# Softmax steps, kept V blocks and w1 row products between two passes over the KV cache

## The chip, the cores and the metric

One core of one Trainium2 chip runs the whole program in one launch. The metric is the device time of that execution in microseconds (us). Five engines have their own instruction streams: PE (matmul; its weight loads are shown as PEld), DVE, ACT, POOL, and SP, which here does nothing but issue loads from DRAM. Stores are issued by POOL.

## The reference

Two attention blocks and two dense blocks alternate on one token, and then the gradients of all of it are taken. The parameters of the two attention blocks are the same arrays, and so are those of the dense blocks:

```python
def _A_ref(x, k_cache, v_cache, wq, wo):          # Hq=32 heads, 4 KV heads, 65536 positions, Dh=128
    q = (x @ wq) ...                               # x: [1, 1, 1024]
    scores = einsum("bhqd,bhkd->bhqk", q, k) * (Dh ** -0.5)
    o = einsum("bhqk,bhkd->bhqd", softmax(scores), v)
    return o.reshape(...) @ wo
def _B_ref(x, w1, b1, w2, b2):                     # 1024 -> 3584 -> 1024
    return relu(x @ w1 + b1) ** 2 @ w2 + b2
...
x = x + _A_ref(_layernorm(x), ...); x = x + _B_ref(_layernorm(x), ...)
x = x + _A_ref(_layernorm(x), ...); x = x + _B_ref(_layernorm(x), ...)
_out, _vjp = jax.vjp(_f, A_x, A_k_cache, A_v_cache, A_wq, A_wo, B_w1, B_b1, B_w2, B_b2)
return (_out, *_vjp(grad_out))
```

All arrays are bf16. K and V are 67 MB each, and the gradients of K and V are as large. The output is right when the values agree; nothing about order is asked for.

## The kernel before

**Four passes over K and V.** The caches do not fit on the chip, so K and V are read once in each of four passes: pass 1 is the attention of the first block, pass 2 that of the second block (`attn_fwd`, with `p` = 0 and 1), pass 3 the backward attention of the second block (`attn_bwd3`, `p` = 2), and pass 4 (`attn_bwd4`, `p` = 3) the backward attention of the first block together with the stores of dK and dV. Between passes lie dense stretches, in which a chain of small steps (output product `wo`, layer norm, `w1`, and so on) must be done before the next pass can use its result.

**The arena.** One SBUF tile of 20 slots of 1 MB holds everything that is loaded. Eight of them (`plane`) come to hold the softmax weights E of two layers and four groups; the other twelve take blocks of K and V, `wo`, `wq`, `w1` and `w2`. `Slot` hands out a free slot when the program is built, `take_pair` a pair for a load of 2 MB. SP issues the loads in the order of the program, and each waits until the last reader of its slot is done; the load behind it in SP's queue waits too.

**Items.** A pass runs over 256 items: 8 chunks of 128 positions each, 256 KB of K and of V. A block (`hb`) is 4 items, 1 MB. `pipeline` walks over the steps and at each step does the stages that are due, each with its lag: in pass 2 K is transposed at lag 0 (`kT`), scores at lag 2 (`kS`), and V is used at lag 36 (`v8`). A unit is 16 items. After the scores of a unit come its softmax steps, made by `stats`, each put some steps later by `after(n, fn)`: `lows` (row minimum, DVE), `turn` (transpose, PE), `low` (DVE), `spread` (PE), `exps` (DVE and ACT), and four times `exp2` (two heads of exponentials each, ACT). `unit_end` folds the unit into the running sum, `group_sum` and `group_out` make the output of the last unit of a group. In pass 3 V is transposed at lag 0 (`vT`), multiplied by dO at lag 2 (`vS`), and K is used at lag 13 (`k8`).

**Kept blocks.** At the end of a pass the first blocks that the next pass needs stay in their slots (`KV["keep"]`, 7 blocks of V from pass 2 to pass 3, 28 items). Four of the seven are blocks that pass 2 has done before its last three: `early_turn` transposes them in place right after `v8` has read them (L1129 to L1134; 16 items), with the copies out of PSUM by ACT and DVE in turn, so that `vT` of pass 3 has nothing to do for them (`is_turned`).

**Between passes 2 and 3.** `g_wo` multiplies by `wo` (L519), `ln_fwd` normalises (L222 to L246), with transposes of `w1` chunk 0 put between its steps by `turn_between`. Then `w1` is worked through in seven chunks of 512 columns (`ch_load`, 1 MB each, 1 KB rows), five of which are loaded ahead. One round of the loop for chunk s is: `ch_fwd(s)`, 32 matmuls and two DVE steps that give `dhb`; `ch_bwd(s-1)`, 20 matmuls; `ch_spread(s)`, 4 matmuls and an ACT copy that spread `dhb` over the partitions; `ch_turn(s+1)`, four times 5 transposes with a copy each (three on ACT, one on DVE; 8 transposes for the last chunk); `ch_dots(s)`, three row products on DVE (L1730); `ch_free(s)` and the next load into that slot. After the rounds come `ln_bwd`, the product with `wo` rows, and pass 3.

The order of instructions on PE, DVE and ACT is the order in the program inside `tc.manual_schedule`.

Of the kernel before, what the change touches and what calls it, by code (L numbers as in the profile page):

```python
# [16 lines left out]
P = 128  # L17
# [3 lines left out]
def kernel(  # L21
# [94 lines left out]
    nc.vector.memset(onesd_f[:], 1.0 / D)  # L116
# [105 lines left out]
    def ln_fwd(x, name, between=lambda n: None, eps=eps_t):  # L222
        s = tmp.tile([P, 1], F32, name="ln_s")
        nc.vector.reduce_sum(out=s[:], in_=x[:], axis=AX.X)
        between(0)
        mean = bcast_sum(s[:], 1, mean=True)
        between(1)
        xc = tmp.tile([P, DC], F32, name="ln_xc")
        negmean = tmp.tile([P, 1], F32, name="ln_negmean")
# [6 lines left out]
        var = bcast_sum(ss[:], 1, mean=True)  # L236
        between(2)
        rstd = vec.tile([P, 1], F32, name=name + "_rstd")
        nc.scalar.activation(out=rstd[:], in_=var[:], func=ACTF.Sqrt, bias=eps[:], scale=1.0)
        nc.vector.reciprocal(out=rstd[:], in_=rstd[:])  # L240
        n = vec.tile([P, DC], F32, name=name + "_n")
        nc.vector.tensor_scalar(out=n[:], in0=xc[:], scalar1=rstd[:, 0:1], scalar2=None, op0=ALU.mult)
        nb = vec.tile([P, DC], BF, name=name + "_nb")
        nc.vector.tensor_copy(out=nb[:], in_=n[:])
        between(3)
        return n, nb, rstd  # L246

    def ln_bwd(dn, n, rstd, between=lambda: None):
# [3 lines left out]
        nc.vector.tensor_tensor(out=pr[:], in0=dn, in1=n[:], op=ALU.mult)  # L252
        nc.vector.reduce_sum(out=st[:, 1:2], in_=pr[:], axis=AX.X)
# [3 lines left out]
        nc.vector.tensor_scalar(out=negm[:], in0=tot[:], scalar1=-1.0, scalar2=None, op0=ALU.mult)  # L257
# [651 lines left out]
    def gsl(g):  # L909
        return slice(g * R, (g + 1) * R)  # L910
# [89 lines left out]
    def attn_fwd(p, L, on_group, bg, end=()):  # L1000
# [56 lines left out]
        def stats(g, su, S, pm):  # L1057
# [52 lines left out]
            for n, fn in ((1, lows), (3, turn), (4, low), (6, spread), (7, exps), (7, exp2(0)), (8, exp2(2)), (9, exp2(4)), (10, exp2(6))):  # L1110
                after(n, fn)

        def v8(g, c8):
# [4 lines left out]
            if c8 % SU == SU // 2 and su != first_su[g]:  # L1118
                t = tmp.tile([P, R], F32, name="o_t")
                nc.vector.tensor_tensor(out=t[:], in0=state[("o", g)][:], in1=state[("al", g, su)][:], op=ALU.mult)  # L1120
                state[("ot", g)] = t
# [7 lines left out]
            if p == 1 and ("v", g, c8 // J) in early_turn:  # L1129
                pt = ps_tr()  # L1130
                for i in range(8):
                    nc.tensor.transpose(pt[:, i, :], vb8[:, i, :], ident_b[:, :])
                evac(vb8[:, :, :], pt[:, :, :], kind="kt" if c8 // 8 % 2 else "kta")
                KV["next"].add(("v", g, c8))  # L1134
# [3 lines left out]
        def unit_end(g, su, ps_o):  # L1138
            on = spool.tile([P, R], F32, name="oacc", tag="oacc", bufs=3)
            rs = state.pop(("rs", g, su))  # L1140
            if su == first_su[g]:
                nc.vector.tensor_copy(out=on[:], in_=ps_o[:, 0, :])
                z2 = rs
            else:
                al = state.pop(("al", g, su))
                nc.vector.tensor_tensor(out=on[:], in0=ps_o[:, 0, :], in1=state.pop(("ot", g))[:], op=ALU.add)
# [4 lines left out]
            state[("o", g)] = on  # L1151
            state[("z", g)] = z2
            if su == last_su[g]:
                after(2, lambda: group_sum(g, z2))
                after(3, lambda: group_out(g, su, on))

        def group_sum(g, z2):
            state["pz"] = bcast_sum(z2[:], R)

        def group_out(g, su, on):  # L1160
            nc.vector.reciprocal(out=L["rZ"][:, gsl(g)], in_=state["pz"][:])
            nc.vector.tensor_tensor(out=L["oT"][:, gsl(g)], in0=on[:], in1=L["rZ"][:, gsl(g)], op=ALU.mult)
            nc.vector.tensor_copy(out=L["oTb"][:, gsl(g)], in_=L["oT"][:, gsl(g)])
# [7 lines left out]
        early_turn = set(k for k in TOUCH[p][:-3] if k in KV["keep"])  # L1171
# [586 lines left out]
    ahead = 0  # L1758
    while ahead < 5 and FREE:
        ch_load(ahead)  # L1760
        ahead += 1
    with tc.manual_schedule(engines=ORDERED):
        run(g_wo(L3, x3, lastg[1], ps_mv, PRE["wo3"]))

        def turn_between(n):
            for s, j, dve in {0: [(0, 0, 0)], 1: [], 2: [(0, 1, 1)], 3: [(0, 2, 0), (0, 3, 1), (1, 0, 0)]}[n]:
                ch_turn(s, [j], {j: dve})
        L4["n"], L4["nb"], L4["rstd"] = ln_fwd(x3, "L4", turn_between, eps4)
        ps_dn = ps_bg([P, DC, 64])
        for s in range(NCH):  # L1770
# [3 lines left out]
            if s < NCH - 1:  # L1774
                ch_spread(s)
                ch_turn(s + 1, [0, 1, 2] if s else [1, 2])
                ch_dots(s)
                ch_turn(s + 1, [3])
            ch_free(s)
            if ahead < NCH:  # L1780
                ch_load(ahead)
                ahead += 1
# [173 lines left out]
```

## Time and profile before

| what | us |
|---|---|
| three timed executions | 1941.15, 1941.16, 1943.75 (median 1941.16) |
| the profiled execution, first to last instruction (span) | 1938.1 |
| busy in it: PE / DVE / ACT / POOL | 1585.2 / 1170.3 / 1044.9 / 142.2 |
| moved by the DMA engines | 787.63 MB, 406 GB/s over the span |

The profiled execution has no other time of its own than its span; the 3 us to the median of the timed runs lie before its first and after its last instruction. In the views, a row of the timeline gives the start in us from the span's start, how long it took, engine, line, operation, what it writes and reads, and in brackets the idle time of the engine before it and what ended that. A row of the windows gives for a stretch its length, the busy time of each engine with the number of instructions, the granted clock of PE, the busy share of the 16 DMA engines (1 and a little over is full) and GB/s. The dense stretch between passes 1 and 2 lies near 345 to 410 us, that between passes 2 and 3 near 740 to 786 us, that between passes 3 and 4 near 1120 to 1220 us.

### The profile page before, as it was taken

Reading aid. Unit: us, or ns where it says so; the run is one execution under the profiler, and the core shown is the slowest. Engines: PE = TensorE matmul, PEld = TensorE weight load, DVE = VectorE, ACT = ScalarE, POOL = GpSimd, SP = SyncE. Lnnn points to the kernel's source line nnn. Section 1 sums busy time; section 2 is a strip of 40 time slices with the busy share of each in tenths; the row PEclk is TensorE's granted clock in tenths of the full one; section 3 lists DMA queues with packets and bytes.
Section 4 is the critical chain, followed back from the end, with each engine's and each line's share of the span. In section 5 each row is a group of like instructions: output and inputs, shape, how many; then the busy total and the mean of one; then the engine's idle time right before and its main releaser. Section 6 shows DMA issues by size and latency. Waiting matters only on the chain. (4 is left out here: it accounts for less than half of the span.)

```text
span 1938.1 us, 66986 instructions
## 1 busy us (share of the span) xinstructions
PE 1585.2 (82%) x30199; PEld 1301.4 (67%) x30199; DVE 1170.3 (60%) x2453; ACT 1044.9 (54%) x1617; POOL 142.2 (7%) x321
## 2 busy tenths in 40 slices
PE   6878778688777888977787898889997987697987
PEld 6878777678777877877776886555554654454554
DVE  5655555255555554545454567777775886685876
ACT  3444334245433545445363455766875885575775
POOL 0000000000000000000000001121111211121211
PEclk9999899689999999998899999898997998797998
DMA  9999999999999998999999988999999999899998
GB/s 393 427 425 425 429 427 415 391 407 423 427 425 429 428 422 309 377 425 429 426 424 421 408 314 308 425 424 389 425 424 413 419 424 424 345 419 397 424 422 352
DMA packets 107149, 787.63 MB, mean 406 GB/s; under 512 B 9440, under 2 KB 16622, under 8 KB 42222
## 3 DMA queue, kind: packets, MB, share of 16 engines
q1 hardware_dynamic: 82782, 617.65, 77.2%
q0 software_dynamic: 24080, 165.70, 20.5%
q8 instruction: 236, 3.87, 0.7%
q14 instruction: 51, 0.42, 0.1%
HBM read 617.62 MB, written 165.69 MB: 404 GB/s over the span
## 5 line engine op out<-in xcount | busy, mean ns | idle before, releaser
L164 DVE COPY kt<-ps_tr 128x1024 bf16<-128x1024 bf16 x724 | 496.3, 688 | 429.0 <-PE ps_tr L1024 244.0
L161 ACT CAST arena<-ps_gg 128x1024 bf16<-128x1024 f32 x457 | 444.4, 1011 | 185.0 <-PE ps_gg L1426 137.9
L1024 PE MATMUL ps_tr<-ident_b,arena 128*128 128x128 bf16 x3840 | 308.2, 225 | 36.9 <-DMA arena<-in_A_k_cache_dram 27.5
L161 ACT COPY kt<-ps_tr 128x1024 bf16<-128x1024 bf16 x164 | 171.0, 1046 | 186.1 <-PE ps_tr L1216 103.3
L164 DVE CAST arena<-ps_gg 128x1024 bf16<-128x1024 f32 (+2 forms) x186 | 222.2, 1195 | 77.1 <-PE ps_gg L1426 34.5
L1024 PEld LDWEIGHTS <-arena 128*128 128x128 bf16 x3840 | 232.9, 101 | 44.7 <-DMA arena<-in_A_k_cache_dram 30.3
L1126 PE MATMUL ps_acc<-arena 128*128 128x64 bf16 (+4 forms) x4096 | 205.6, 196 | 60.2 <-DMA arena<-in_A_v_cache_dram 45.1
L1426 PE MATMUL ps_gg<-GG,xt 64*128 64x512 bf16 x1024 | 210.6, 409 | 43.3 <-DVE arena L164 28.3
L1345 PE MATMUL ps_tr<-ident_b,arena 128*128 128x128 bf16 x1824 | 177.4, 232 | 33.7 <-DMA arena<-in_A_v_cache_dram 30.7
L1126 PEld LDWEIGHTS <-arena 128*128 128x128 bf16 x4096 | 159.9, 100 | 66.1 <-DMA arena<-in_A_v_cache_dram 48.7
L1042 PE MATMUL ps_sc<-L_qpad,kt 128*128 128x64 bf16 (+7 forms) x3584 | 183.0, 194 | 16.3 <-issue 8.3
L1107 ACT ACTIVATE arena<-S_sb,L_negm 128x128 bf16<-128x128 f32 x256 | 165.5, 1002 | 55.7 <-DVE L_negm L1092 42.2
L1216 PE MATMUL ps_tr<-ident_b,arena 128*128 128x128 bf16 x1920 | 154.3, 226 | 44.3 <-DMA arena<-in_A_v_cache_dram 43.5
L1345 PEld LDWEIGHTS <-arena 128*128 128x128 bf16 x1824 | 116.8, 103 | 90.7 <-issue 55.2
L1042 PEld LDWEIGHTS <-kt 128*128 128x128 bf16 x3584 | 152.6, 100 | 20.2 <-issue 8.8
L1216 PEld LDWEIGHTS <-arena 128*128 128x128 bf16 x1920 | 117.1, 101 | 48.8 <-DMA arena<-in_A_v_cache_dram 46.1
L1457 PEld LDWEIGHTS <-arena 128*128 128x128 bf16 x2048 | 92.2, 101 | 57.8 <-issue 39.9
L1107 ACT ACTIVATION_READ_ACCUMULATOR arena<-S_sb,L_negm 128x1 f32 x256 | 127.9, 500 | 0.0
L1426 PEld LDWEIGHTS <-xt 64*128 64x128 bf16 x1024 | 64.5, 94 | 90.1 <-issue 52.3
L587 ACT ACTIVATE mv_t<-mv_t 128x1024 bf16<-128x1024 bf16 x96 | 102.1, 1065 | 35.8 <-DVE mv_t L598 35.8
L1382 PE MATMUL ps_sc<-DOB,kt 128*128 128x64 bf16 (+3 forms) x1824 | 112.3, 197 | 0.1
L1270 PE MATMUL ps_acc<-dsT,arena 128*128 128x64 bf16 (+7 forms) x2048 | 103.1, 194 | 11.3 <-DMA arena<-in_A_k_cache_dram 7.8
(317 smaller groups left out, 2154.0 us busy)
## 6 DMA issues: line engine op xcount, KB each, us to landing
arena<-in_A_k_cache_dram SPq DMA_DIRECT2D x82, 2048.0 KB, 21.7
arena<-in_A_v_cache_dram SPq DMA_DIRECT2D x79, 2048.0 KB, 21.7
out_dram<-arena POOLq DMA_DIRECT2D x149, 1024.0 KB, 16.2
arena<-in_A_v_cache_dram SPq DMA_DIRECT2D x84, 1024.0 KB, 14.2
arena<-in_A_k_cache_dram SPq DMA_DIRECT2D x84, 1024.0 KB, 14.6
arena<-in_A_wo_dram SPq DMA_DIRECT2D x22, 1024.0 KB, 19.6
arena<-in_B_w_dram SPq DMA_DIRECT2D x21, 1024.0 KB, 9.2
arena<-in_A_wq_dram SPq DMA_DIRECT2D x18, 1024.0 KB, 18.0
```

Source lines behind the costliest of these rows:

```text
L161: nc.scalar.copy(out=out, in_=in_)
L164: nc.vector.tensor_copy(out=out, in_=in_)
L587: nc.scalar.activation(out=t[:, :], in_=t[:, :], func=ACTF.Copy, accum_out=y[:, kc:kc + 1])
L1024: nc.tensor.transpose(pt[:, i, :], kb8[:, i, :], ident_b[:, :])
L1042: nc.tensor.matmul(state["ps_s"][:, s:s + w, :].rearrange("p a b -> p (a b)"), lhsT=kt[:, i, :], rhs=L["qpad"][:, g, 0:w, :].rearrange("p ...
L1107: nc.scalar.activation(out=E(p, g, c0, SU)[:, :, h], in_=S[:, h, :], func=ACTF.Exp, bias=L["negm"][:, g, su, h:h + 1], scale=SCALE, accum_ ...
L1126: nc.tensor.matmul(ps_o[:, 0:w, :], lhsT=vb8[:, i, :], rhs=E(p, g, c, w), start=(c % SU == 0), stop=(c % SU == SU - 1), skip_group_check=True)
L1216: nc.tensor.transpose(pt[:, i, :], vb8[:, i, :], ident_b[:, :])
L1270: nc.tensor.matmul(ps_dq[:, 0:w, :].rearrange("p a b -> p (a b)"), lhsT=kb8[:, i, :], rhs=dsT[:, s:s + w, :].rearrange("p a b -> p (a b)") ...
L1345: nc.tensor.transpose(pt[:, i, :], vb8[:, i, :], ident_b[:, :])
L1382: nc.tensor.matmul(state["ps_dp"][:, s:s + w, :].rearrange("p a b -> p (a b)"), lhsT=vt[:, i, :], rhs=DOB[:, g, 0:w, :].rearrange("p a b - ...
L1426: nc.tensor.matmul(pg[:, 512 * h:512 * h + 512], lhsT=xt[64 * h:64 * h + 64, j1 // 8 + m, :], rhs=gg[64 * h:64 * h + 64, :, :].rearrange(" ...
```

## The change

The softmax steps of the last unit of a forward pass are due 1, 2, 2, 3, 3, 3, 4, 4 and 5 steps after its scores (before: 1, 3, 4, 6, 7, 7, 8, 9, 10). The sum of the softmax is folded in the middle of a unit's `v8` (`unit_sums`) and `group_out` follows `unit_end` at once; the bf16 output is multiplied directly. The transposes of kept V blocks in pass 2 are gone; two items of block 0 are transposed between the passes (`turn_kept`). In the loop over `w1`, the row products, the freeing of the slot and the next load belong to the chunk before, and one piece of `ch_turn` stands ahead of `ch_spread`. In the layer norms two DVE steps are merged into one with an accumulator, and the sign of the mean goes into the constant.

```diff
-    nc.vector.memset(onesd_f[:], 1.0 / D)
+    nc.vector.memset(onesd_f[:], -1.0 / D)
...
-        nc.vector.tensor_scalar(out=negmean[:], in0=mean[:], scalar1=-1.0, scalar2=None, op0=ALU.mult)
-        nc.vector.tensor_scalar(out=xc[:], in0=x[:], scalar1=negmean[:, 0:1], scalar2=None, op0=ALU.add)
+        nc.vector.tensor_tensor(out=xc[:], in0=x[:], in1=negmean[:, 0:1].to_broadcast([P, DC]), op=ALU.add)
...
-        nc.vector.tensor_tensor(out=sq[:], in0=xc[:], in1=xc[:], op=ALU.mult)
-        nc.vector.reduce_sum(out=ss[:], in_=sq[:], axis=AX.X)
+        nc.vector.scalar_tensor_tensor(out=sq[:], in0=xc[:], scalar=1.0, in1=xc[:], op0=ALU.mult, op1=ALU.mult, accum_out=ss[:])
...
-            for n, fn in ((1, lows), (3, turn), (4, low), (6, spread), (7, exps), (7, exp2(0)), (8, exp2(2)), (9, exp2(4)), (10, exp2(6))):
+            at = (1, 2, 2, 3, 3, 3, 4, 4, 5) if (g, su) == last_unit else (1, 3, 4, 6, 7, 7, 8, 9, 10)
+            for n, fn in zip(at, (lows, turn, low, spread, exps, exp2(0), exp2(2), exp2(4), exp2(6))):
                 after(n, fn)
...
-            if p == 1 and ("v", g, c8 // J) in early_turn:
-                pt = ps_tr()
-                for i in range(8):
-                    nc.tensor.transpose(pt[:, i, :], vb8[:, i, :], ident_b[:, :])
-                evac(vb8[:, :, :], pt[:, :, :], kind="kt" if c8 // 8 % 2 else "kta")
-                KV["next"].add(("v", g, c8))
...
+            if c8 % SU == SU // 2:
+                unit_sums(g, su)
...
-                after(2, lambda: group_sum(g, z2))
-                after(3, lambda: group_out(g, su, on))
+                after(2, lambda: group_sum(g, z2))
+        def unit_end(g, su, ps_o):
...
+            if last:
+                group_out(g, su, on)
...
+    def turn_kept(c8, dve=False):
+        g = firstg[2]
+        vb8 = kv8("v", g, c8)
+        pt = ps_tr()
+        for i in range(8):
+            nc.tensor.transpose(pt[:, i, :], vb8[:, i, :], ident_b[:, :])
+        (nc.vector.tensor_copy if dve else nc.scalar.copy)(out=vb8[:, :, :], in_=pt[:, :, :])
+        KV["next"].add(("v", g, c8))
     with tc.manual_schedule(engines=ORDERED):
+        turn_kept(ITEMS[2][0][1])
         run(g_wo(L3, x3, lastg[1], ps_mv, PRE["wo3"]))
         def turn_between(n):
+            if n == 0:
+                turn_kept(ITEMS[2][1][1])
...
             if s < NCH - 1:
+                first = 1 - min(s, 1)
+                ch_turn(s + 1, [first])
                 ch_spread(s)
-                ch_turn(s + 1, [0, 1, 2] if s else [1, 2])
-                ch_dots(s)
-                ch_turn(s + 1, [3])
-            ch_free(s)
-            if ahead < NCH:
-                ch_load(ahead)
-                ahead += 1
+            if s:
+                ch_dots(s - 1)
+                ch_free(s - 1)
+                ch_next()
+            if s < NCH - 1:
+                ch_turn(s + 1, range(first + 1, 4))
+        ch_free(NCH - 1)
```

The same number of bytes is loaded in the same number of loads. Since slots are handed out while the program is built, the changed order of steps also changes which slot some loads get: the second load of `wq` after the dense stretch between passes 1 and 2, one load of 2 MB before, is now two of 1 MB.

More of the change, by code (lines that the diff above doesn't have):

```diff
@@ L256, in ln_bwd @@
         negm = tmp.tile([P, 2], F32, name="lnb_negm")
-        nc.vector.tensor_scalar(out=negm[:], in0=tot[:], scalar1=-1.0, scalar2=None, op0=ALU.mult)
+        nc.vector.tensor_copy(out=negm[:], in_=tot[:])
         t = tmp.tile([P, DC], F32, name="lnb_t")
@@ L1170, in attn_fwd @@
         start_pass(p)
-        early_turn = set(k for k in TOUCH[p][:-3] if k in KV["keep"])
+        last_unit = (items[-1][0], items[-1][1] // SU)
         n = len(items) // G
```

52 lines of the change are left out of this document (27 added, 25 removed).

## Prediction

> **What bounds the kernel now.** First the page's row of DMA share by slices: the transfers run nearly all the time, so whatever the engines save counts only where that row drops.
>
> ```profile
> span 1938.1 us, 66986 instructions
> DMA  9999999999999998999999988999999999899998
> ```
>
> Two drops belong to dense stretches that the change touches: slices 15 and 16 (727 to 824 us; the rows below place them) and, too short for a slice, one near 408 us. The windows give them their size.
>
> ```profile
> core 0: us, PE busy (x) PEld busy (x) DVE busy (x) ACT busy (x) POOL busy (x), PEclk, DMA share, GB/s
> 406.00:410.00 4.00, 2.72 (x55) 2.33 (x52) 2.08 (x13) 2.21 (x3) 0.61 (x13) 1.00 0.69 258
> 716.00:736.00 20.00, 16.23 (x397) 15.39 (x394) 9.76 (x24) 15.22 (x37) 0.00 (x0) 1.00 1.00 414
> 736.00:744.00 8.00, 7.21 (x195) 7.05 (x194) 2.55 (x7) 5.51 (x9) 0.00 (x0) 1.00 0.82 276
> 744.00:756.00 12.00, 8.16 (x155) 7.33 (x155) 3.96 (x22) 4.05 (x7) 0.00 (x0) 0.87 1.05 360
> 756.00:760.00 4.00, 3.35 (x80) 3.23 (x78) 2.56 (x9) 2.01 (x4) 0.00 (x0) 0.98 0.30 89
> 760.00:786.00 26.00, 23.39 (x550) 22.57 (x548) 19.02 (x72) 15.53 (x23) 0.00 (x0) 1.00 0.88 289
> 786.00:814.00 28.00, 25.72 (x606) 23.83 (x606) 11.33 (x23) 8.13 (x9) 0.00 (x0) 0.94 1.00 416
> 814.00:826.00 12.00, 11.84 (x291) 11.13 (x290) 8.48 (x16) 8.49 (x13) 0.00 (x0) 1.00 0.91 363
> ```
>
> Until 736 and from 744 to 756 the transfers are full; from 756 to 786 they moved 4 x 89 + 26 x 289 = 7.9 MB, which at the 416 GB/s of the next row takes 18.9 us of the 30. So up to 11 us can be had there, by GB/s (5.9 us by the share). There the loads wait for slots that the chain of the dense stretch frees one at a time; from 786 on the transfers bind again, so a chain that ends x us earlier shifts the rest of the run by about x. I follow that chain in the timeline.
>
> ```profile
> 730.66 0.21 ACT L1097 ACTIVATE al<-df 128x8 f32<-128x8 f32 x1 [1.08 <-DVE df L1095]
> 736.44 0.61 PE L1132 MATMUL ps_tr<-ident_b,arena 128*128 128x128 bf16 x8 [1.81 <-ACT arena L161]
> 737.23 0.50 ACT L1107 ACTIVATION_READ_ACCUMULATOR arena<-S_sb,L_negm 128x1 f32 x1
> 745.68 0.17 DVE L1146 TENSOR_TENSOR oacc<-ps_acc,o_t 128x8 f32<-128x8 f32 x1 [3.04 <-PE ps_acc L1126]
> 747.11 0.17 DVE L1163 CAST L_oTb<-L_oT 128x8 bf16<-128x8 f32 x1
> 747.34 2.15 PE L519 MATMUL ps_mv<-L_oTb,arena 128*128 128x64 bf16 x64 [0.70 <-DVE L_oTb L1163]
> 749.32 0.44 PE L1712 MATMUL ps_tr<-ident_b,arena 128*128 128x128 bf16 x5
> 750.03 0.35 PE L212 MATMUL ps_mv<-ln_s,onesd_f 128*128 128x1 f32 x2 [0.26 <-DVE ln_s L224]
> 753.10 1.87 PE L1738 MATMUL ps_sc<-L_nb,arena 128*128 128x64 bf16 x32
> 779.60 0.17 DVE L1795 COPY dn<-ps_bg 128x8 f32<-128x8 f32 x1 [0.51 <-PE ps_bg L1752]
> 781.19 0.34 PE L212 MATMUL ps_mv<-lnb_st,onesd_f 128*128 128x2 f32 x2
> ```
>
> The last unit's exponentials share ACT with the copies of kept V (PE waits 1.81 us for one), the unit ends at 745.68, its bf16 output at 747.28, the `wo` product runs from 747.34, the first layer-norm sum from 750.03, the rounds from 753.10 to 779.60 (26.5 us).
>
> **Term 1: up to the first round.** Gone from pass 2 are 16 x 8 transposes and 16 copies; the softmax steps move ahead. Even with exponentials that ended no earlier than now (737.7), the last unit would end when its V is there. What V and `wo` allow is in the view of issues to landing (the last number of a row), asked for the two issues of `wo` at 721.48 and 725.31 and that of chunk 2 at 742.24:
>
> ```profile
> arena<-in_A_wo_dram SPq DMA_DIRECT2D x1, 1024.0 KB, 20.9
> arena<-in_A_wo_dram SPq DMA_DIRECT2D x1, 1024.0 KB, 19.6
> arena<-in_B_w_dram SPq DMA_DIRECT2D x1, 1024.0 KB, 10.9
> ```
>
> `wo` lands at 742.4 and 744.9, 2.5 us apart; the last V half, ahead of it in SP's order, near 740. Chunk 2 lands at 753.1; chunk 0, two places ahead, between 744.9 and 753.1, by equal steps of 2.7 us at 747.7. So the unit can end near 741 and its output is no longer last: `wo` is, then chunk 0. PE takes its instructions in order, and ahead of the layer-norm sum stand 5 transposes of chunk 0, and now 8 of a kept item (0.45 us by the row at 817 below). The sum then starts at 747.7 + 0.3 + 0.45 = 748.5 instead of 750.03: -1.5. In the norm the negation goes and two steps become one; small DVE steps last 0.16 to 0.17 us, and some waiting goes with them: -0.35. Term: -1.85. Bounds: -0.4 (chunk 0 at 749.2, the norm alone gained) and -4 (chunk 0 right behind `wo`).
>
> **Term 2: the rounds.**
>
> ```profile
> 764.13 0.69 DVE L1730 SCALAR_TENSOR_TENSOR mv_junk<-arena,wvb 128x512 bf16<-128x512 bf16 x1 [1.15 <-ACT wvb L1723]
> 765.02 1.22 PE L1738 MATMUL ps_sc<-L_nb,arena 128*128 128x64 bf16 x32
> 765.97 0.48 DVE L1714 COPY wt<-ps_tr 128x640 bf16<-128x640 bf16 x1
> 766.07 0.78 PE L1752 MATMUL ps_bg<-dhb,wt 128*128 128x64 bf16 x20
> 766.56 0.16 DVE L1742 SCALAR_TENSOR_TENSOR dhb<-ffn_h,dg4x 128x4 bf16<-128x4 f32 x1
> 766.78 0.40 PE L1721 MATMUL ps_acc<-ident_b,dhb 128*128 128x128 bf16 x4
> 767.01 1.00 PE L1712 MATMUL ps_tr<-ident_b,arena 128*128 128x128 bf16 x15
> 768.49 0.44 PE L1712 MATMUL ps_tr<-ident_b,arena 128*128 128x128 bf16 x5 [0.47 <-ACT wt L1714]
> 768.77 1.23 PE L1738 MATMUL ps_sc<-L_nb,arena 128*128 128x64 bf16 x32
> ```
>
> A round is 768.77 - 765.02 = 3.75 us, and it goes round through DVE: `dhb`, spread, ACT copy, row products (1.84 us from 764.13 to 765.97), copy, `dhb`. With the products a round later that circle is cut, and PE's own work is left: forward 1.05 (to the next start), backward 0.65 (20 at 0.032), 20 transposes at 0.056 = 1.12, spread 0.23: 3.05. The transposes put ahead of the spread cover the wait for `dhb` (766.72 - 765.02 = 1.7 after the round's start; spread now at 1.05 + 0.65 + 0.28 = 1.98). DVE has 0.36 + 1.84 + 0.48 = 2.7, ACT three copies and the spread's, some 2.5: both fit. Round 0 saves 5 transposes, 3.75 to 3.45 (its forward was slow, 1.87); rounds 1 to 4 are 3.05; round 5 has 12 transposes more, 3.7. Sum 19.35. In round 6 the products of chunk 5 now come behind `dhb`: 1.9 + 1.85 + 0.4 until `dn` is copied = 4.15. Together 23.5 instead of 26.5: -3.0. Behind it 32 transposes of `wo` held PE until 781.19; PE now reaches them while DVE does the products, and the sum follows `dn` after some 0.7 us instead of 1.59: -0.9. Term: -3.9. Bounds -1.9 (rounds of 3.4, should ACT's copies set the pace) and -4.5. The slot of a chunk is freed a round later, but at the end of the products of a shorter round: chunk 5 is issued near 758.8, as before; no round waits for it.
>
> **Term 3: the head of pass 3.** 14 more items are transposed in pass 3 (16 not in pass 2, two in the dense stretch).
>
> ```profile
> 816.28 0.33 SPq L370 DMA_DIRECT2D arena<-in_A_k_cache_dram  x1
> 817.02 0.61 PE L1216 MATMUL ps_tr<-ident_b,arena 128*128 128x128 bf16 x8
> 817.47 0.40 PE L1242 MATMUL ps_sc<-dOpad,kt 128*128 128x64 bf16 x8
> 829.77 0.62 PE L1216 MATMUL ps_tr<-ident_b,arena 128*128 128x128 bf16 x8 [2.63 <-DMA arena<-in_A_v_cache_dram]
> 407.11 0.37 SPq L462 DMA_DIRECT2D arena<-in_A_wq_dram  x1
> ```
>
> An item's transposes hold PE for 817.47 - 817.02 = 0.45 us; the copies go to ACT and DVE, busy 8 and 11 of 28 us there. Items 2 and 3 fall into the wait for dO, so 12 x 0.45 = 5.4 us on PE; slots of V and K come free later, and SP's queue stands behind them. PE waited 2.63 us for V at 829.77, so at most 5.4 - 2.63 = 2.8 reaches the transfers; below, 0, since they were full until 814 with loads queued. I take +1.4, the middle. The load of K at 816.28 gets another pair of slots, which it can have 4 items earlier; that is why not more.
>
> **Term 4: elsewhere.** Near 408 us the second load of `wq` was one of 2 MB and waited for the last slab of `w2` (issued 407.11), loads of K and V behind it in SP's queue. As two of 1 MB its first half waits for the fourth slab, and three loads go out earlier. The idle there is 0.31 x 4 = 1.2 us: -1.2 (bounds 0 and -1.2). The three `ln_bwd` behind pass 3 lose a step of 0.16: -0.3. Transposes taken from pass 2 itself, at full transfers, are worth nothing; without that cover they would be 16 x 0.45 = 7 us.
>
> **Sum.** -1.85 - 3.9 + 1.4 - 1.5 = -5.85: span 1932.3, and with the 3.1 us by which the median stands above the span, 1935.4.
>
> **Rivals.** *A: PE late at the head of pass 3.* PEclk is 0.94 in 786:814, and the forward of 753.10 took 1.87 instead of 1.22, so PE does slow down at times. If it does so for these items, 5.4 us become 8.3 to 10.8, DMA drains behind SP's queue, and less 2.63 some 7 are lost; with bounds of terms 1, 2 and 4 (-0.4 - 1.9 - 0.3) the sum is about +4.5: 1945.5. It decides when the 12 items cost over 0.65 us each. Against: full transfers until 814. *B: the transfers bind the stretch.* Chunks land later, rounds wait for them, only the end and term 4 are gained: -2, 1939.2. For: 360 GB/s on 1 KB rows; against: 89 GB/s at 756. *C: a cold start of the rounds.* PE waits from 741 to 747.7 with only 64 matmuls between; if its work up to the second round then takes 1.87/1.22 as long and more, 3 us of it cost 1.7 more: 1937.1. The Trainium skill, "TensorE: Matmul & The Clock Gate", part 1 on the HAM clock gate, says that PE falls to half its clock after an idle window of about 3.4 us and that the windows run freely; the 0.87 of 744:756 agrees. *D: the last unit's PE steps, now close together, hold V back.* They do, but V lands near 740 anyway; then nothing.
>
> **How the numbers follow.** A measurement of this kernel tells 0.2% (3.9 us) from no change. The forecast has 0.55, C 0.13, B 0.18, A 0.14. Faster (under 1937.3): 0.55 and most of C, 0.66; slower (over 1945.0): most of A, 0.12; the rest 0.22. Best bounds together give 1932, worst without A 1941; A's lower half takes the range to 1943.
>
> **What would show it.** First round from 751.3, dn near 774.7 counted from the same end of pass 2; rounds 3.05 apart; no dip at 408; DMA share in the 30 us before pass 3 above 0.9. Wrong, if rounds stay at 3.7, or if a new dip near 810 is over 3 us.

## The result and the profile after

The changed kernel took 1937.51 us (median of 12 runs, 1935.05 to 1942.51) and the kernel before, in as many runs, 1941.98 us (1940.47 to 1946.61): a ratio of 0.9977, 95% interval 0.9967 to 0.9987. The prediction was 1935.4 us, in a range from 1932 to 1943. The interval excludes a ratio of 1, but the median stands 0.2 us above the 1937.3 us from which the prediction counts the kernel as faster. Two later repeats of the changed kernel, each beside the kernel before, gave 0.9970 (0.9960 to 0.9981) and 0.9969 (0.9957 to 0.9980). The profiled execution took 1935.05 us with a span of 1933.2 us.

First the same windows as before, of the changed kernel (columns as there):

```profile
406.00:410.00 4.00, 2.44 (x48) 2.21 (x46) 1.81 (x12) 1.55 (x3) 0.61 (x13) 0.90 1.04 421
736.00:744.00 8.00, 4.48 (x99) 4.11 (x99) 1.05 (x7) 1.72 (x3) 0.00 (x0) 0.77 0.93 319
744.00:756.00 12.00, 11.09 (x218) 10.51 (x216) 5.49 (x22) 7.17 (x12) 0.00 (x0) 0.87 0.96 322
756.00:760.00 4.00, 3.95 (x104) 3.85 (x101) 3.22 (x12) 2.60 (x5) 0.00 (x0) 1.00 0.87 275
760.00:786.00 26.00, 25.06 (x568) 23.85 (x566) 20.50 (x73) 14.05 (x18) 0.00 (x0) 1.00 0.98 355
786.00:814.00 28.00, 26.38 (x644) 24.90 (x640) 13.98 (x24) 11.26 (x12) 0.00 (x0) 1.00 1.01 412
814.00:826.00 12.00, 10.20 (x259) 9.65 (x257) 8.43 (x15) 9.14 (x14) 0.00 (x0) 1.00 0.92 367
```

The drop at 408 us is gone (421 GB/s, 258 before). In the dense stretch 756 to 760 went from 89 to 275 GB/s and 760 to 786 from 289 to 355. By the busy share, 760 to 786 is now nearly full (0.98), although it moves 355 GB/s there and 412 behind it (1.01). So of the prediction's two figures for what could be had, 11 us by GB/s and 5.9 us by the share, it was the second that counted. No new hole stands at 814. The chain of the stretch in the timeline of PE, with the three rows of DVE that matter at its end:

```profile
740.30 1.89 PE L515 MATMUL ps_mv<-L_oTb,arena 128*128 128x64 bf16 x32 [1.41 <-DMA arena<-in_A_wo_dram]
743.17 1.89 PE L515 MATMUL ps_mv<-L_oTb,arena 128*128 128x64 bf16 x32 [0.98 <-DMA arena<-in_A_wo_dram]
746.30 0.53 PE L212 MATMUL ps_mv<-ln_s,onesd_f 128*128 128x1 f32 x2
749.16 1.23 PE L1736 MATMUL ps_sc<-L_nb,arena 128*128 128x64 bf16 x32
751.63 1.23 PE L1736 MATMUL ps_sc<-L_nb,arena 128*128 128x64 bf16 x32
754.88 1.23 PE L1736 MATMUL ps_sc<-L_nb,arena 128*128 128x64 bf16 x32
768.48 1.22 PE L1736 MATMUL ps_sc<-L_nb,arena 128*128 128x64 bf16 x32
772.06 0.16 DVE L1812 COPY dn<-ps_bg 128x8 f32<-128x8 f32 x1
775.18 2.22 PE L710 MATMUL ps_bg<-vcb,arena 128*128 128x64 bf16 x64
777.89 0.69 DVE L164 COPY kt<-ps_tr 128x1024 bf16<-128x1024 bf16 x1
778.57 0.15 DVE L1222 CAST dOpad<-L_dOT 128x8 bf16<-128x8 f32 x1
778.77 0.40 PE L1240 MATMUL ps_sc<-dOpad,arena 128*128 128x64 bf16 x8 [0.68 <-DVE dOpad L1222]
```

Both halves of `wo`'s product now wait for the load of `wo`, no longer for the last unit; from the second round on the w1 rounds are 3.25 us apart (754.88 - 751.63); and the first score product of pass 3 waits for a cast on DVE that stands behind a copy of 0.69 us.

To see where the time came from, the traces are laid over each other by loads: the moment at which the same number of megabytes had been loaded, minus that moment in the kernel before (us; below zero is earlier). The last row is the span.

| loaded | before at | changed | second run | third run | what lies ahead of it |
|---|---|---|---|---|---|
| 168 MB | 405.8 | -1.0 | -1.1 | -1.2 | most of the stretch between passes 1 and 2 |
| 170 MB | 412.2 | -2.5 | -2.6 | -2.7 | the drop at 408 |
| 290 MB | 696.3 | -2.4 | -1.9 | -2.2 | nearly all of pass 2 |
| 306 MB | 734.2 | -1.4 | -1.5 | -1.6 | the last loads of pass 2 |
| 325 MB | 796.2 | -7.0 | -6.2 | -6.4 | the stretch between passes 2 and 3 |
| 340 MB | 833.9 | -6.3 | -4.7 | -5.3 | the head of pass 3 |
| 460 MB | 1120.0 | -6.0 | -4.6 | -5.0 | the rest of pass 3 |
| all | 1938.1 | -4.9 | -0.5 | -3.7 | pass 4, where single executions scatter by some us |

### The profile page after: what moved, and what is told of

Its sections match the earlier page's. It is cut to its first block, busy times and chain, and to the rows that moved or that the text cites. A ratio compares the mean times of both kernels' runs of the same rounds, so it can differ in the third digit from the quotient of the medians.

```text
span 1933.2 us, 66962 instructions
## 1 busy us (share of the span) xinstructions
PE 1588.5 (82%) x30199; PEld 1304.0 (67%) x30199; DVE 1173.3 (61%) x2451; ACT 1042.0 (54%) x1615; POOL 141.8 (7%) x321
## 5 line engine op out<-in xcount | busy, mean ns | idle before, releaser
L164 DVE COPY kt<-ps_tr 128x1024 bf16<-128x1024 bf16 x734 | 504.4, 689 | 425.6 <-PE ps_tr L1020 238.2
L1020 PE MATMUL ps_tr<-ident_b,arena 128*128 128x128 bf16 x3840 | 312.6, 227 | 45.4 <-DMA arena<-in_A_k_cache_dram 30.8
L1020 PEld LDWEIGHTS <-arena 128*128 128x128 bf16 x3840 | 234.9, 101 | 53.6 <-DMA arena<-in_A_k_cache_dram 32.8
L161 ACT COPY kt<-ps_tr 128x1024 bf16<-128x1024 bf16 x168 | 176.7, 1056 | 171.1 <-PE ps_tr L1214 108.8
L1343 PE MATMUL ps_tr<-ident_b,arena 128*128 128x128 bf16 x1824 | 177.4, 232 | 30.2 <-DMA arena<-in_A_v_cache_dram 27.5
L1214 PE MATMUL ps_tr<-ident_b,arena 128*128 128x128 bf16 x2032 | 163.6, 226 | 40.0 <-DMA arena<-in_A_v_cache_dram 37.0
L1121 PEld LDWEIGHTS <-arena 128*128 128x128 bf16 x4096 | 160.1, 101 | 53.8 <-DMA arena<-in_A_v_cache_dram 37.5
L1343 PEld LDWEIGHTS <-arena 128*128 128x128 bf16 x1824 | 116.8, 103 | 87.6 <-issue 55.6
L1214 PEld LDWEIGHTS <-arena 128*128 128x128 bf16 x2032 | 123.6, 101 | 45.4 <-DMA arena<-in_A_v_cache_dram 39.6
L1455 PEld LDWEIGHTS <-arena 128*128 128x128 bf16 x2048 | 92.2, 101 | 56.3 <-issue 38.5
```

The source lines that it names most:

```text
L161: nc.scalar.copy(out=out, in_=in_)
L164: nc.vector.tensor_copy(out=out, in_=in_)
L1020: nc.tensor.transpose(pt[:, i, :], kb8[:, i, :], ident_b[:, :])
L1121: nc.tensor.matmul(ps_o[:, 0:w, :], lhsT=vb8[:, i, :], rhs=E(p, g, c, w), start=(c % SU == 0), stop=(c % SU == SU - 1), skip_group_check=True)
```

## The experiments

All 14 profiles, of 11 kernels, in one table first. The second to the sixth column are from one profile each: the first round of w1 against before (after taking off the lead at 306 MB); six rounds, from the first forward to the last; from there to the product with `wo` rows; from that to the first score product of pass 3; and what the head of pass 3 takes or gives after it, until 340 MB are loaded. For each profile the differences to before in these columns, with its lead at 306 MB, add up to its lead at 340 MB. The last column is the ratio of the timed runs to the kernel before on the same chip, with its interval.

| kernel | first round | six rounds | to the product | to the score | head | ratio |
|---|---|---|---|---|---|---|
| before | 0 | 23.65 | 6.42 | 2.77 | 0 | 1 |
| changed | -2.5 | 19.32 | 6.70 | 3.59 | +0.9 | 0.9977 (0.9967 to 0.9987) |
| changed, second run | -1.9 | 19.70 | 6.69 | 3.59 | +1.5 | 0.9970 (0.9960 to 0.9981) |
| changed, third run | -1.8 | 19.77 | 6.70 | 3.59 | +0.9 | 0.9969 (0.9957 to 0.9980) |
| before, wq split | +0.3 | 23.66 | 6.45 | 2.77 | 0.0 | 0.9985 (0.9971 to 0.9999) |
| before, products late | +1.8 | 20.51 | 7.35 | 3.29 | +0.3 | 0.9989 (0.9977 to 1.0001) |
| changed, products back | -2.1 | 23.49 | 6.43 | 3.53 | +3.7 | 0.9995 (0.9985 to 1.0005) |
| changed, kept V back | +0.1 | 19.32 | 7.04 | 4.67 | -0.7 | 0.9968 (0.9955 to 0.9980) |
| changed, steps back | -1.9 | 19.96 | 6.70 | 3.59 | +1.5 | 0.9973 (0.9963 to 0.9983) |
| changed, sum first | -2.2 | 20.00 | 6.70 | 3.59 | +1.0 | 0.9982 (0.9972 to 0.9992) |
| the same, repeated | -2.2 | 20.00 | 6.70 | 3.59 | +2.4 | 0.9972 (0.9958 to 0.9986) |
| changed, four items | -2.1 | 20.35 | 6.70 | 2.84 | +1.2 | 0.9964 (0.9953 to 0.9975) |
| changed, kept V by DVE | -2.7 | 19.98 | 6.75 | 4.36 | -1.2 | 0.9964 (0.9952 to 0.9975) |
| kept V by DVE, four items | -2.1 | 19.57 | 7.22 | 3.85 | -0.5 | 0.9953 (0.9936 to 0.9971) |

**The load of wq alone**, in the kernel before (`whole` is true for this one load):

```diff
-            if ks and flat and NOW["wide"] and not odd_one():
+            if ks and flat and NOW["wide"] and not odd_one() and not whole(name):
```

> The kernel before with one thing changed: the second load of wq between passes 1 and 2 is two loads of 1 MB instead of one of 2 MB, as in the changed kernel; layer norms, softmax steps, kept V and w1 rounds stay as before. Theory: the drop in transfers near 408 us comes from that load, which waits for the last slab of w2 with the loads of K and V behind it. Then 406 to 410 us moves about 420 GB/s instead of 258 and pass 2 runs 1.2 to 1.5 us earlier; the span is 1936.6 to 1937. Rival: the shorter layer norm does it (its output is 0.4 us earlier). Then the drop at 408 us stays and the span is 1938. Second rival: the gain is given back when pass 2 meets its own limit (in the changed kernel 0.9 us of it was gone by 703 us); then the span is within 0.5 us of 1938.

Its window at the place of the drop:

```profile
406.00:410.00 4.00, 2.52 (x50) 2.13 (x46) 2.26 (x14) 2.22 (x3) 0.61 (x13) 1.00 1.03 413
```

The drop is that load: 413 GB/s without touching the layer norm, and a lead of 2.0 us at 170 MB (0.4 of it already there at 168 MB). In this profile 1.5 us of the lead were lost again before 484 us, and its span is 1939.0, above the 1936.6 to 1937 expected, so the second rival has a part; the timed runs keep a gain whose interval (0.01 to 0.29%) holds the predicted 1.2 us.

**The rounds alone, both ways.** In the kernel before, the order of the changed kernel's loop; in the changed kernel, the order of before:

```diff
-                ch_turn(s + 1, [first])
-                ch_spread(s)
-            if s:
-                ch_dots(s - 1)
-                ch_free(s - 1)
-                ch_next()
-            if s < NCH - 1:
-                ch_turn(s + 1, range(first + 1, 4))
-        ch_free(NCH - 1)
+                ch_spread(s)
+                ch_turn(s + 1, [0, 1, 2] if s else [1, 2])
+                ch_dots(s)
+                ch_turn(s + 1, [3])
+            ch_free(s)
+            ch_next()
```

> The kernel before with only the order in the w1 rounds changed: row products, freeing and next load one round later, one piece of the transposes ahead of the spread. Theory: the rounds leave the circle through DVE and are set by PE alone; they shrink from 3.75 to 3.24 us as in the changed kernel, the copy of dn comes 3.3 to 3.7 us earlier (counted from the first round), the layer-norm backward behind it gains nothing because 64 transposes of wo rows (about 4 us of PE) still stand there, and the span is 1934.5 to 1935.5. Rival: the rounds can only shrink because chunk 0 and the first round come earlier; with the first round at 753.1 the later chunks are waited for and rounds stay at 3.5 or more: span 1936.5 to 1937.5.

> The changed kernel with the row products back in their own round (the order of the w1 rounds as before), all else as changed. Theory: rounds of 3.75 us, first round still near 749, dn 3.3 to 3.7 us later than in the changed kernel (near 775.5), and 2.5 to 3.5 us on the span: about 1936.3. Rival: the w1 chunks or loads set the pace there, and the span is within 1 us of the changed kernel's 1933.2.

Forwards on PE with the products late in the kernel before, then two forwards, and PE's longest wait at the head of pass 3 with its windows, with the products back in the changed kernel:

```profile
755.40 1.78 PE L1738 MATMUL ps_sc<-L_nb,arena 128*128 128x64 bf16 x32
759.06 1.23 PE L1738 MATMUL ps_sc<-L_nb,arena 128*128 128x64 bf16 x32
762.30 1.23 PE L1738 MATMUL ps_sc<-L_nb,arena 128*128 128x64 bf16 x32
```

```profile
761.72 1.23 PE L1736 MATMUL ps_sc<-L_nb,arena 128*128 128x64 bf16 x32
765.47 1.23 PE L1736 MATMUL ps_sc<-L_nb,arena 128*128 128x64 bf16 x32
...
806.37 0.39 PE L1268 MATMUL ps_acc<-dsT,arena 128*128 128x64 bf16 x8 [1.88 <-issue]
```

```profile
806.00:816.00 10.00, 9.63 (x204) 8.98 (x204) 4.41 (x8) 2.37 (x3) 0.00 (x0) 0.83 0.89 355
816.00:826.00 10.00, 10.00 (x232) 8.96 (x228) 6.92 (x12) 7.37 (x12) 0.00 (x0) 1.00 0.85 297
```

The order of the loop alone makes a round 3.24 (762.30 - 759.06) or 3.75 us (765.47 - 761.72), wherever it stands: the rival that chunks or loads set the pace falls. Taken out of the changed kernel, it takes 0.18 to 0.26% of time with it (0.9995 against 0.9977, 0.9970 and 0.9969; 3.5 to 5.1 us of 1942); the interval of 0.9995 lies clear of those of the two repeats and touches that of the first runs. Put into the kernel before, it is not shown to bring anything (0.9989, up to 1.0001): its rounds give 3.1 us, and 0.9, 0.5 and 0.3 of that are lost again up to the product, up to the score and at the head, with two waits marked `issue` of 0.75 and 0.36 us on the way. The single spans missed their expectations: 1945.8 with the products late (a first round of 3.66 us, half a clock from 755.6 to 759.0, and most of the rest lost in pass 4), 1938.9 with them back, where PE stood for 1.88 us at the head of pass 3, ran at a clock of 0.83, and the transfers fell to 297 GB/s.

**Kept V back in pass 2, softmax steps early:**

```diff
             kv_done("v", g, c8)
+            if p == 1 and ("v", g, c8 // J) in early_turn:
...
+                evac(vb8[:, :, :], pt[:, :, :], kind="kt" if c8 // 8 % 2 else "kta")
...
-        turn_kept(ITEMS[2][0][1])
...
-            if n == 0:
-                turn_kept(ITEMS[2][1][1])
```

> The changed kernel with the 16 items of kept V again transposed in pass 2 right after their use, as before, and none between the passes; the softmax steps of the last unit stay early. Theory: the head of pass 3 loses nothing any more (the changed kernel loses 0.6 us against before between 790 and 830 us), but the copies on ACT stand between the exponentials of the last unit again; the unit's end stays ahead of wo's landing or at most 1 us behind it: span 1932.5 to 1934. Rival A: the 14 items moved cost more than they show, since they also hold up the slots in pass 3: span under 1931.5. Rival B: the copies delay the exponentials so far that wo's product starts 2 us or more later: span over 1935.

From its timelines, ACT and then PE:

```profile
734.79 1.04 ACT L1103 ACTIVATE arena<-S_sb,L_negm 128x128 bf16<-128x128 f32 x1
735.36 3.13 ACT L161 COPY arena<-ps_tr 128x1024 bf16<-128x1024 bf16 x3
```

```profile
736.74 0.61 PE L1127 MATMUL ps_tr<-ident_b,arena 128*128 128x128 bf16 x8 [1.31 <-ACT arena L161]
748.23 2.15 PE L515 MATMUL ps_mv<-L_oTb,arena 128*128 128x64 bf16 x64 [0.46 <-DVE L_oTb L1166]
753.61 1.23 PE L1743 MATMUL ps_sc<-L_nb,arena 128*128 128x64 bf16 x32
```

The span is 1940.7, over the 1935 of rival B, and rival B holds for the place: with kept V back, `wo` starts at 748.23 and the first round is where it was in the kernel before (+0.1), early steps or not. It is PE that is late there (16 x 0.45 = 7.2 us of transposes between the products with V, and waits for their copies), not the exponentials: the last of these starts at 734.79, and from 736.74 to the unit's end PE has no wait above 0.26 us. But the head of pass 3 gets back 0.7 us instead of losing 0.9 to 1.5, and the timed ratio, 0.9968, is that of the changed kernel: the move out of pass 2 is worth nothing that these runs can tell. (The 4.67 us to the score holds a wait marked `issue` of 1.72 us; without it, it is 2.95.)

**The second run of the changed kernel, and the steps back:**

> The changed kernel itself once more, beside the next three on one chip, so that they are compared with it and not only with the kernel before. Theory: the ratio to before is again near 0.9977 (0.9967 to 0.9987 so far), and the profile shows the same landmarks: first forward of w1 four us behind the second half of wo's product, rounds 3.24 us apart. Rival: what differs from run to run (waits for instructions, PE's clock) moves single profiles by 1 to 5 us, as in the runs with the row products late and the kept blocks back; then this profile's span differs from 1933.2 by over 2 us while the rounds and the order of events are the same.

```diff
-            at = (1, 2, 2, 3, 3, 3, 4, 4, 5) if (g, su) == last_unit else (1, 3, 4, 6, 7, 7, 8, 9, 10)
+            at = (1, 3, 4, 6, 7, 7, 8, 9, 10)
```

> The changed kernel with the softmax steps of the last unit at their old places (1, 3, 4, 6, 7, 7, 8, 9 and 10 steps behind its scores), all else as changed. Theory: without kept V on ACT the exponentials would have been early enough; they end some 2 to 4 us later than in the changed kernel, the unit's end is still near or before the landing of wo's halves (740.0 and 743.1), so the first round is at most 1 us later and the span within 1 us of the changed kernel. Rival: the early steps are what ended the wait at the unit's end; then wo's product starts 2 us or more later, the first round too, and the time is 2 us or more above the changed kernel's.

```profile
742.09 1.17 PE L515 MATMUL ps_mv<-L_oTb,arena 128*128 128x64 bf16 x32 [1.41 <-DMA arena<-in_A_wo_dram]
744.60 1.89 PE L515 MATMUL ps_mv<-L_oTb,arena 128*128 128x64 bf16 x32 [1.34 <-DMA arena<-in_A_wo_dram]
```

The second run bears out the ratio and the landmarks, and also that a single span means little: 1937.6. With the steps back, PE waits for `wo` no less (1.41 and 1.34 us, 1.41 and 0.98 in the changed kernel), the unit ends at the same distance from the loads, and the ratio is the same: the earlier softmax steps bring nothing. Its span, 1935.4, is 2.2 us above 1933.2, where 1 us was expected; the timed runs show no such difference.

**The layer-norm sum first, twice:**

```diff
-            if n == 0:
+            if n == 1:
                 turn_kept(ITEMS[2][1][1])
-            for s, j, dve in {0: [(0, 0, 0)], 1: [],
+            for s, j, dve in {0: [], 1: [(0, 0, 0)],
```

> The changed kernel with one matmul moved: the first layer-norm sum stands ahead of the transposes of the kept item and of chunk 0 on PE instead of behind them. Theory: in the changed kernel PE did 13 transposes from 744.88 while the sum's input was there at 745.46; the sum comes 0.8 us earlier, the first forward of w1 0.5 to 0.8 us earlier after wo's second half, and the time falls by about as much, less than these runs can tell. Rival: chunk 0, which lands at 745.7, and the transposes of it set the first round; then the distance from wo's second half to the first forward stays within 0.2 us.

> The run with the layer-norm sum first, repeated unchanged, for one question: in its first profile PE stood still for 2.00 us at 416.07 in the first scores of pass 2, waiting for nothing that the profile shows, while the changed kernel stood there for at most 0.80 us, and the 2.3 us gained near 408 us were gone by 446 us. Theory: the wait comes with the program (where its instructions lie), not with the run; it is 2.00 us again and the gain is again gone by 446 us. Rival: it comes by chance from run to run; then it is 0.5 to 0.8 us in this profile, and the gain near 408 us stays.

The first run's wait in the scores of pass 2, then the repeat's:

```profile
416.07 4.73 PE L1038 MATMUL ps_sc<-L_qpad,arena 128*128 128x64 bf16 x111 [2.00 <-issue]
```

```profile
415.13 3.34 PE L1038 MATMUL ps_sc<-L_qpad,arena 128*128 128x64 bf16 x111 [0.81 <-issue]
```

The sum itself came earlier (0.54 us after the end of `wo`'s product instead of 1.24), but from the end of that product to the first forward it was 4.78 us in both runs, against 4.10, 4.84 and 4.82: nothing gained, and the rival holds against two of the three. The wait of 2.00 us marked `issue`, for instructions as the last section shows, came by chance: 0.81 in the repeat, where a lead of 1.8 us stayed, while the first run had none left at 484 us. The profiles of kept V back and of steps back have a wait of 2.00 us near 416 us too, and just these three have no lead left at 484 us (0.0 to 0.1 us late); the eight others of the changed kernel and its variants still have 1.2 to 3.2 us there.

**Kept V by DVE, four items, and both; the third run of the changed kernel:**

The first edit is that of kept V by DVE, which besides turns the first two items of block 0 ahead of `wo`'s product and has the layer-norm sum first; the second is that of four items; the kernel with both has the layer-norm sum first, too.

```diff
+            if p == 1 and ("v", g, c8 // J) in early_turn and (g, su) != last_unit:
...
+                nc.vector.tensor_copy(out=vb8[:, :, :], in_=pt[:, :, :])
```

```diff
-        turn_kept(ITEMS[2][0][1])
+        for k in range(4):
+            turn_kept(ITEMS[2][k][1])
```

> The changed kernel with 12 items of kept V (blocks 4 to 6) transposed in pass 2 again, but with their copies on DVE so that ACT's exponentials are not held up; the four items of block 0 as in the changed kernel (two turned between the passes), and the layer-norm sum first. Theory: PE has 6 us of waits between 731 and 743 us in the changed kernel, which take 12 x 0.45 = 5.4 us of transposes; wo's product ends within 1 us of where it did, the head of pass 3 has 12 transposes less, and the time is 0.5 to 1.5 us below the changed kernel's. Rival: the chain through the last unit ends 2 us or more later, as with the kept blocks back; then the time is equal to the changed kernel's or above.

> The changed kernel a third time, as the reference on this chip for the next two. Theory: ratio to before 0.996 to 0.999, rounds of 3.24 us, 3.6 us from the start of the product with wo rows to the first score product of pass 3.

> The changed kernel with all four items of kept block 0 transposed before wo's product (PE waits there for wo) instead of one before and one after it. Theory: in the changed kernel the third item's transposes and their 0.69 us copy stand on DVE ahead of dO's cast, which the first score product of pass 3 waits for: 3.59 us from the start of the product with wo rows to it, against 2.77 before. With items 2 and 3 already turned it is 2.8 to 2.9 again, the first layer-norm sum comes 0.5 us earlier as well, and the time is 1 to 1.5 us below the changed kernel's. Rival: the wait for dO is not set by that copy; then the distance stays at 3.4 us or more and only the 0.5 us is gained. Second rival: the extra transposes hold wo's product up by over 0.5 us; then nothing is gained.

> The best version so far (12 items of kept V transposed in pass 2 with copies on DVE, layer-norm sum first) with all four items of block 0 transposed before wo's product as well, so that pass 3 begins as in the kernel before. Theory: 2.8 us from the start of the product with wo rows to the first score product (4.36 with 0.64 of it a wait for instructions in the run with two items), wo's product at most 0.5 us later; ratio to before 0.9955 to 0.9965. Rival: PE is full between 725 and 742 us there, so the two items more push wo's product and the first round by 0.9 us; then the ratio stays at that of the run with two items (0.9964) or above.

Four items, from the product with `wo` rows to the first score product; then the version with both, its windows in the stretch and its waits at the head of pass 3:

```profile
776.55 2.22 PE L710 MATMUL ps_bg<-vcb,arena 128*128 128x64 bf16 x64
779.39 0.64 PE L1240 MATMUL ps_sc<-dOpad,arena 128*128 128x64 bf16 x16
```

```profile
736.00:744.00 8.00, 6.26 (x172) 5.95 (x170) 1.78 (x8) 3.85 (x4) 0.00 (x0) 1.00 0.90 301
744.00:756.00 12.00, 10.45 (x242) 9.76 (x243) 5.06 (x23) 6.39 (x12) 0.00 (x0) 1.00 1.01 346
...
796.00:806.00 10.00, 6.71 (x184) 6.20 (x181) 1.56 (x4) 2.02 (x2) 0.00 (x0) 1.00 1.01 424
```

```profile
745.30 2.15 PE L515 MATMUL ps_mv<-L_oTb,arena 128*128 128x64 bf16 x64 [0.46 <-DVE L_oTb L1166]
750.68 1.23 PE L1743 MATMUL ps_sc<-L_nb,arena 128*128 128x64 bf16 x32
...
792.91 0.35 PE L1275 MATMUL ps_acc<-dsT,arena 128*128 128x64 bf16 x6 [0.99 <-issue]
798.57 0.38 PE L1275 MATMUL ps_acc<-dsT,arena 128*128 128x64 bf16 x7 [1.42 <-issue]
805.34 0.62 PE L1221 MATMUL ps_tr<-ident_b,arena 128*128 128x128 bf16 x8 [1.87 <-issue]
```

With four items turned the score product stands 2.84 us behind the product (779.39 - 776.55), near the 2.77 of before: the copy on DVE was the wait. The layer-norm sum did not come earlier, against what was expected: it starts 1.25 us behind the end of `wo`'s product (1.23 in the third run), since PE waits 0.73 us there for chunk 0. The median is 0.7 us under the changed kernel's on the same chip (1936.97 against 1937.66), and 2.1 us under it with kept V by DVE alone (1936.33 against 1938.38); the intervals overlap in both cases.

With both, PE's waits of 0.99, 1.42 and 1.87 us at the head of pass 3 cost hardly any transfers (424 GB/s from 796 to 806 us, 428 in the 10 us behind it), while in the run with the products back 355 and 297 GB/s stand beside one of 1.88 and a low clock. That 12 transposes less leave PE the room is argued from this. Up to the score it was to be 2.8 us again and is 3.85, 0.90 of it a wait marked `issue` within the product. Both together have the lowest median of all (1934.81 us of 6 runs, ratio 0.9953), 2.9 us under the changed kernel on the same chip; but the intervals overlap, so only that it beats the kernel before is shown. `wo`'s product was to start at most 0.5 us later and started 3.9 later (745.6 against 741.7 in the changed kernel, leads at 306 MB taken off): PE was full, as the rival said. (With kept V back, as many transposes but half of their copies on ACT, it started at 747.8, so those copies have a part in the delay there.) But it then had both halves of `wo`, ended 1.3 us later only, and the first round came no later.

## Why the prediction came out

**Its sum.** At the head of pass 3's end the prediction has -1.85 - 3.9 + 1.4 - 1.2 = -5.55 us; the three profiles have -6.3, -4.7 and -5.3. The median fell by 4.5 us in the first runs, and the two repeats by 0.30 and 0.31% (5.8 and 6.0 us) for a predicted 5.8. The forecast case was the right one: each term came out within 0.9 us, and their errors partly cancel. Inside the terms some steps were off.

Of the 3.1 us by which the prediction puts the median above the span, 1.7 to 1.9 us lie outside the span: by so much the time stands above its own span in every execution on record (1935.05 and 1933.2 us here). The rest is that the profiled execution of the kernel before was shorter than the median one. The forecast of 5.8 us between two medians does not hang on it. The prediction's best bounds together (-4 - 4.5 - 1.5) give 1931 and not 1932.

**Term 1 (-1.85) held in size, -2.5, -1.9 and -1.8, with one cause too many.** The unit's end, near 741 predicted, is at 738.93, 740.35 with the lead taken off; `wo` and chunk 0 are last, as said. Removing the transposes does it (+0.1 with them back); the softmax steps do nothing (-1.9 without them). What the term left out, and rival C has, is the clock: after PE's waits for `wo` the first forward is 4.10 to 4.84 us behind the end of its product, and 3.23 with PE kept busy (750.68 - 747.45); 20 transposes on that way took 1.46 us in the first run, where the clock was full again from 747.1, and 2.29 in the third, where it was not before 751.0.

**Term 2 (-3.9): right in size and cause, with errors that cancel.** From the first forward to the product with `wo` rows the three runs have -4.05, -3.68 and -3.60. To the last forward the prediction had 23.65 us become 19.35, and 19.32, 19.70 and 19.77 came; but a steady round is 3.24 and not 3.05, as the 20 transposes of a round took 1.34 us (753.32 to 753.60 and 753.82 to 754.88) and not 1.12, and round 0 was shorter (2.47 to 2.96 for 3.45): two errors that nearly cancel. Behind the last forward the prediction has `dn` 1.3 us later (4.15 for 2.85) and the layer-norm sum 0.9 closer behind it. It was 0.73 (772.06 - 768.48 = 3.58) and 0.71 (0.88 us for 1.59), so the sum stands where it stood. The -0.9 is thus no gain: in the kernel before, PE has work without a break from the last forward to the product (6.42 us, 64 transposes of `wo` rows among it), and 6.42 became 6.70. That step looked at which wait ends and not at what PE still had to do.

**Term 3 (+1.4): 1.7 to 2.3 came, in another place.** "Items 2 and 3 fall into the wait for dO" was the wrong step: their transposes do, but the copy of the third item stands on DVE ahead of the cast of dO and costs 3.59 - 2.77 = 0.8 us, which four items turned earlier take away. Behind it the head costs 0.9 to 1.5. Rival A, PE late at the head of pass 3, did not come in the changed kernel's own profiles; one variant showed it (+3.7), beside a wait for instructions of 1.88 us and a clock of 0.83; which of them set it off was not tried.

**Term 4 (-1.2 up to here, -1.5 in all): -1.4 to -1.6 at the end of pass 2, in other pieces.** The drop gave 1.5, and 1.6 with the split alone. Another 1.0 to 1.2 was there before it, of which the split has 0.4; the rest may be the shorter layer norm, which was not tried alone. Some 0.4 to 1 us was lost again among the last loads of pass 2, where one load waits longer in SP's queue than in the kernel before:

```profile
686.12 0.33 SPq L366 DMA_DIRECT2D arena<-in_A_v_cache_dram  x1
697.88 0.33 SPq L366 DMA_DIRECT2D arena<-in_A_k_cache_dram  x1
```

Before, the load of K went at 694.00, 6.1 us behind the one of V and not 11.8; with the split alone it is 6.1 us as well. That the other handing out of slots does this was only argued. That the gain of the drop was still there at all is partly luck: three profiles of variants, which have the same split, lost it behind a single wait of 2.00 us near 416 us. The -0.3 for the layer norms behind pass 3 can't be seen in the scatter of pass 4.

**Rivals B to D.** B, transfers binding the stretch, is out: the rounds shrank whole. But little is left under that bound: the loads between 306 and 325 MB gained 4.7 to 5.6 us of the 5.9 that the share had free. C came in part: the clock was 0.77 and 0.87 in the two windows from 736 to 756 (0.71 in the latter in the third run), and the way from `wo` to the first round is 0.9 to 1.6 us longer than at a clock of 1.00, which the earlier start paid. D held: PE waited for V twice (1.33 us at 735.38 and 1.13 at 737.84), but `wo` landed later still.

## What to carry to other kernels

Where a wait is removed, count what is left on the engine behind it before booking the gain: the rounds gave it, the layer norm behind them did not, since PE had 64 transposes to do there in any case. Try the parts of a change one by one: here the order of the loop and the split load carry what the times show, the kept blocks and the softmax steps nothing that they show, and the shorter layer norm and the earlier fold of the softmax sum were not tried alone. Work moved off one place is not free at the next because an engine idles there: look at what its copy is queued ahead of, and at what the idle time was covering (waits for instructions at the head of pass 3). And effects of 1 us are read from distances between landmarks in several profiles, since single spans of one and the same kernel here went from 1933.2 to 1937.6 us.

## What the runs showed of the hardware

PE stands still again and again while the transfers are nearly full, waiting for nothing that the profile names (`issue`). In the changed kernel's timeline at the head of pass 3:

```profile
817.31 0.33 PE L1214 MATMUL ps_tr<-ident_b,arena 128*128 128x128 bf16 x3 [0.69 <-issue]
823.80 0.28 PE L1240 MATMUL ps_sc<-dOpad,kt 128*128 128x64 bf16 x4 [1.11 <-issue]
```

and on its page, in the DMA queues (packets, MB, share of the engines), the queue that loads instructions, 16 KB a packet; then the same queue from 821.37 to 822.35 us, ahead of the second wait:

```profile
q8 instruction: 236, 3.87, 0.7%
q8 instruction: 1, 0.02, 6.1%
```

PE and PEld have 30199 instructions each on that page, together 256 a packet. That the waits are for these packets can be read from the traces: in all 14 profiles each of the 619 waits of this kind above 0.5 us ends 1.2 to 1.7 us behind the end of such a packet, where only some 6% of moments taken at random would. The changed kernel has 44 of them, 44.6 us in all; 43 come behind 4 us with a DMA share of 0.9 or more. What makes one longer than another stays open: one lasted 0.81 us in one run and 2.00 in another of the same program, and there the whole lead of 2.5 us was gone.

The granted clock falls although PE is never idle for long: with waits of 1.41 and 0.98 us around 32 matmuls it was 0.77 from 736 to 744 us, and half of `wo`'s product took 1.89 us; with PE busy 6.26 of the 8 us it was 1.00, and the whole product took 2.15. The Trainium skill, "TensorE: Matmul & The Clock Gate", part 1, tells of windows of about 3.4 us that run freely and of half the clock after an idle one. The lengths agree: the clock was at 0.50 for 3.41 us in the kernel before (from 752.77), and for 6.8, 10.2 and 13.7 us in the three profiles of the changed one (from 740.29, 740.53 and 737.31). That it starts at another place in each run of one program fits windows that don't start with the kernel, as does the scatter of round 0 (2.47, 2.86 and 2.96 us). The 0.87 that the prediction names is one such window at half clock. An idle window ahead of it is not what the rows show. Before, then changed:

```profile
749.36:752.77 3.41, 2.21 (x33) 1.90 (x30) 1.76 (x9) 1.43 (x3) 0.00 (x0) 1.00 1.04 348
752.77:756.18 3.41, 2.94 (x45) 2.62 (x43) 0.96 (x5) 1.02 (x3) 0.00 (x0) 0.50 1.05 364
```

```profile
733.47:736.88 3.41, 1.90 (x54) 1.66 (x50) 0.37 (x2) 0.48 (x1) 0.00 (x0) 1.00 0.87 303
736.88:740.29 3.41, 1.06 (x32) 0.97 (x32) 0.51 (x4) 0.76 (x2) 0.00 (x0) 1.00 0.92 342
```

The clock fell behind a stretch with 2.21 us of work in the one and behind one with 1.06 in the other, and did not fall behind one with 1.90. So a longer busy time does not by itself keep the clock up, and what the chip counts stays open.
